# A state-space layer beside a Mish feed-forward: the third block's second product by seven quarter products over 16 of its 28 K tiles

## The chip, the core and the metric

The kernel runs on one core of a Trainium2 chip. The metric is the device time of one execution in microseconds (us), the median of several runs. Everything below is the work of five engines with one instruction queue each: PE (TensorE, matrix products, with PEld for its weight loads), DVE (VectorE), ACT (ScalarE), POOL (GpSimd, here mostly an issuer of DMAs) and SP (SyncE, an issuer of DMAs). The engines wait for one another through semaphores. PSUM, where PE accumulates, has eight banks of 128 x 512 float32.

## The reference, cut to what matters

```python
xn  = layernorm(x)                                  # x: 2048 x 1024, bf16
# S5: a diagonal complex recurrence over the 2048 rows
Bu  = xn @ B_bar.T;   h[t] = Lam_bar * h[t-1] + Bu[t]
y   = 2 * real(h @ C.T) + xn * Dskip
# feed-forward with Mish, F = 3584
hid = xn @ w1 + b1;   act = hid * tanh(softplus(hid))
out = x + y + act @ w2
```

`act @ w2` is called dense 2 here. Its K dimension is F = 3584, that is 28 K tiles of 128.

## The kernel before, in words

**Blocks.** The 2048 rows are worked in four blocks (`blk` 0 to 3) of 512 rows. Each block has three stages on PE: the products that make `hid` and the recurrence's input (L853, L929, L1001, L1361), dense 2 (L1415, in the last block L1472), and the projection of the recurrence's states by C (L1415 with `hT` as operand, L1438, L1446). All eight PSUM banks hold one block's output, 4 groups of 128 rows (`q`) by 2 halves of 512 columns (`h`): bank 2q + h. Dense 2 and the projection accumulate into the same banks, and DVE then adds the block's rows of x and puts the result into `xx` (L1545, L1541), which ACT sends out (L1531).

**Dense 2 in blocks 0 to 2.** For each K tile, eight matmuls of 128 x 128 by 128 x 512, one for each bank: 224 in a block. A ring of seven slots of 512 KB holds the right operands. SP loads it by a list (`items`): a slot gets the item seven places on as soon as PE (`item_done`) is through with it. A w2 item holds two K tiles, so it feeds 16 matmuls.

**Dense 2 in the last block.** There the product is done by seven quarter products (a Winograd form of Strassen's scheme) over K tile pairs: rows of the block are halved (th) and so are K (tile k and tile k + 14, "hi") and the columns. `KIND` = (1, 7, 2, 5, 6, 3, 4) is their order. Products 1, 2 and 4 take quarters of `act` as they are, products 5, 6, 7 and 3 take sums of quarters (S1, S2, S3, S4; `act_sums`, L1291, on DVE in float16). The right operands are quarters of w2 and sums of them (L1206, DVE); those are made once, group by group (`d2_load` L1173, `d2_row`/`d2_scale` L1186 on ACT, `d2_store` L1178 by POOL), where a group `g` is K tiles 2g, 2g + 1 and their partners, and go through DRAM (`w2d`). Seven groups make 28 K tiles. So that the float16 sums are in range, rows of w2 are scaled by powers of two (`row_sizes` L1222 and `row_powers` L1228 to L1232 find them), act by their inverses times a global power (`act_scale` L882; `row_bound`, `row_most`, `row_scales` find it through DRAM), and the states by the global power (L1389). ACT puts products 1, 7, 5 and 6 aside into `KS` (`keep`, L1483), and the end adds them back.

**What orders the work.** Every engine runs its queue in program order. For the first stages of blocks 1, 2 and 3 that order is written out by hand in the strings `WHOLE`, `STEPS` and `LAST`: two-letter steps, of which `p` to `z` are the products of w1 (`w_product`, `w_evacuate` with L1021 on ACT, L1024 and L1038 on DVE), `a` to `d` those of B, `r` the rotation of the states into the recurrence's frame (L891, L897, L899), `g` Mish (`mish`, L876), `k` one pending sum of w1 or w2 (L1151, L1206), `u` a first part of dense 2, `G` an `act_scale` of two tiles, `t` act sums, `m` and `h` load and scale w2 groups, `S` `row_scales`, `l` loads the next block's x. The recurrence (`recur`) then runs j = 0 to 7 on DVE: two scans (L1377), a rotation (L891) and two sums (L1384, L1386).

**The statistics of the next block's rows** (`next_stats`, `next_root`, `next_scale`) run on ACT during the recurrence, and SP transposes the result into `xnT` (`transpose_dma`).

## Time and profile before

| | |
|---|---|
| median of 3 runs | 591.79 us (591.69 to 592.7) |
| span of the profiled execution | 589.9 us (the page gives this span as its own time; the median lies 1.9 us above it) |
| PE busy | 586.5 us, 99% |
| DVE, ACT, POOL busy | 494.2, 384.6, 159.9 us |
| mean granted TensorE clock | 1.000 |
| block 2 on PE: first stage, dense 2, projection | 307.0 to 373.5, to 422.7, to 450.3 us |
| block 3 on PE: first stage, dense 2, projection | 450.3 to 516.7, to 559.9, to 587.7 us |

The times of the blocks are starts of the matmul groups in the trace, from the start of the span. A row of the timeline reads: start, length, engine, line, operation, out<-in, partitions x elements and type, count, and in brackets how long the engine was idle before it and who ended that.

### The profile page before, as it was taken

The numbers are of one execution on the slowest core, as the hardware profiler recorded it, in microseconds if no ns is written. First come the engines' busy times: TensorE is split into PE (matmuls) and PEld (weight loads), VectorE is DVE, ScalarE is ACT, GpSimd is POOL, SyncE is SP. The second block draws the span as 40 slices with busy tenths as digits, with TensorE's granted clock in tenths as the row PEclk, the third lists the DMA queues.
The fourth block names the chain that finished last, engine by engine and source line by source line (L and its number), as shares of the span: only waits on it lengthen the run. The fifth ranks groups of instructions, "written<-read, shape, count | busy, mean of one in ns | idle before, by whom it ended". The sixth has DMA issues, their size and how long they took to land.

```text
span 589.9 us, 9744 instructions
## 1 busy us (share of the span) xinstructions
PE 586.5 (99%) x3651; PEld 355.8 (60%) x3651; DVE 494.2 (84%) x730; ACT 384.6 (65%) x517; POOL 159.9 (27%) x225
## 2 busy tenths in 40 slices
PE   9999999999999999999999999999999999999998
PEld 8644444444447887444458888644446888844444
DVE  6999788999898778989737867998598669789996
ACT  4839994579577775992706477898342798892420
POOL 2899300213752213400302511144210123100000
PEclk9999999999999999999999999999999999999999
DMA  8999999997799688968869959999897966989832
GB/s 255 298 242 245 229 193 231 314 384 222 212 371 306 247 287 302 319 221 213 274 230 380 408 183 295 350 331 276 304 270 263 393 246 233 331 307 334 290 120 71
DMA packets 115993, 161.90 MB, mean 274 GB/s; under 512 B 56010, under 2 KB 67018, under 8 KB 115946
## 3 DMA queue, kind: packets, MB, share of 16 engines
q1 hardware_dynamic: 96768, 104.42, 59.3%
q0 software_dynamic: 14112, 46.28, 22.9%
q10 hardware_dynamic: 5066, 10.57, 5.0%
q8 instruction: 29, 0.48, 0.4%
q14 instruction: 18, 0.15, 0.1%
HBM read 115.09 MB, written 34.08 MB: 253 GB/s over the span
## 4 chain that ended last, share of the span: by engine, by line
PE 98%; DMA 1%; SPq 1%; DVE 0%; issue 0%
PE ps L1415 43%; PE ps L1001 19%; PE ps L929 12%; PE ps L853 10%; PE ps L1472 7%; PE ps L1361 5%; DMA ring<-in_B_w_dram 1%; PE ps L672 1%; PE ps L663 0%; PE ps L1438 0%; SPq L397 0%; PE ps L1446 0%; PE ps L505 0%; SPq L447 0%; SPq L401 0%; DVE xx L1572 0%
## 5 line engine op out<-in xcount | busy, mean ns | idle before, releaser
L1415 PE MATMUL ps<-ring,act 128*128 128x512 bf16 x672 | 145.9, 379 | 0.0
L1415 PEld LDWEIGHTS ps<-ring,act 128*128 128x128 bf16 x672 | 65.7, 98 | 78.4
L1021 ACT ACTIVATE snaps<-ps,par,cs 128x256 f32<-128x256 f32 x98 | 53.4, 562 | 54.4 <-PE ps L1001 29.3
L1415 PE MATMUL ps<-ring,hT 128*128 128x512 bf16 x370 | 80.3, 379 | 0.0
L1001 PE MATMUL ps<-TT,ring 128*128 128x256 f16 x576 | 71.2, 273 | 0.0
L891 DVE TENSOR_TENSOR mt<-hT,tab 128x2048 bf16<-128x2048 bf16 (+1 forms) x56 | 68.5, 1223 | 1.4
L1415 PEld LDWEIGHTS ps<-ring,hT 128*128 128x128 bf16 x370 | 36.2, 98 | 43.7
L1178 POOL DMA_DIRECT2D w2d<-hb x42 | 29.9, 714 | 117.2 <-DVE hb L1206 71.2
L1001 PEld LDWEIGHTS ps<-TT,ring 128*128 128x128 f16 (+1 forms) x576 | 56.2, 98 | 7.5 <-issue 0.2
L1038 DVE SCALAR_TENSOR_TENSOR act<-ps,cs,snaps 128x512 bf16<-128x512 f32 x54 | 40.1, 749 | 23.1 <-PE ps L1001 21.3
L1377 DVE TENSOR_TENSOR_SCAN hT<-cs,qi,hT 128x512 bf16<-128x512 f32 x48 | 58.9, 1269 | 0.0
L853 PE MATMUL ps<-xnT,ring 128*128 128x512 bf16 x264 | 57.3, 379 | 0.0
L1001 PE MATMUL ps<-xnT,ring 128*128 128x256 bf16 x432 | 54.5, 273 | 0.0
L1001 PEld LDWEIGHTS ps<-xnT,ring 128*128 128x128 bf16 (+1 forms) x432 | 42.3, 98 | 5.3
L853 PEld LDWEIGHTS ps<-xnT,ring 128*128 128x128 bf16 x264 | 25.8, 98 | 30.9
L876 ACT ACTIVATE act<-act 128x2048 bf16<-128x2048 bf16 (+3 forms) x12 | 32.8, 2756 | 6.9 <-DVE act L1024 6.8
L1130 POOL DMA_DIRECT2D wsd<-hb x35 | 18.9, 543 | 59.4 <-DVE hb L1151 35.1
L954 DVE TENSOR_TENSOR hT<-ps,snaps 128x512 f16<-128x512 f32 x36 | 23.9, 688 | 12.5 <-ACT snaps L946 10.2
L1136 ACT ACTIVATE hb<-hb,cs 128x2048 bf16<-128x2048 bf16 x10 | 19.4, 1993 | 19.9 <-DVE cs L1125 13.5
L861 ACT ACTIVATE act<-ps,par 128x512 bf16<-128x512 f32 (+1 forms) x40 | 23.9, 654 | 10.5 <-PE ps L853 10.5
L1361 PE MATMUL ps<-xnT,BT 128*128 128x512 bf16 x128 | 27.8, 379 | 0.0
L1415 PE MATMUL ps<-CT,hT 128*128 128x512 bf16 x128 | 27.8, 379 | 0.0
(223 smaller groups left out, 988.9 us busy)
## 6 DMA issues: line engine op xcount, KB each, us to landing
ring<-wsd SPq DMA_DIRECT2D x126, 256.0 KB, 5.3
ring<-in_B_w_dram SPq DMA_DIRECT2D x62, 512.0 KB, 5.6
ring<-ctd SPq DMA_DIRECT2D x24, 512.0 KB, 4.6
ring<-w2d SPq DMA_DIRECT2D x24, 512.0 KB, 4.7
w2d<-hb POOLq DMA_DIRECT2D x42, 256.0 KB, 5.2
wsd<-hb POOLq DMA_DIRECT2D x35, 256.0 KB, 5.1
hb<-in_B_w_dram POOLq DMA_DIRECT2D x20, 256.0 KB, 5.6
ctd<-CT ACTq DMA_DIRECT2D x8, 512.0 KB, 6.4
```

Of the source, the lines that this page charges most:

```text
L853: PE.mm(lambda e, k=k, w=w: e.matmul(ps[:, bank, :], lhsT=w, rhs=xnT[:, k, :], start=k == 0, stop=k == NK - 1), reads=[b_ring[s]] + b_xnT, ...
L876: aop(lambda e: e.activation(t, t, AF.Mish), reads=b, writes=b)
L891: vop(lambda e: e.tensor_tensor(mt[:], u.unsqueeze(1).to_broadcast([P, 2, 2, TB]), tab[:, :, j, :].unsqueeze(2).to_broadcast([P, 2, 2, TB] ...
L929: PE.mm(lambda e, w=w, x=x, o=o, begin=begin, end=end: e.matmul(ps[:, bank, o:o + TH], lhsT=w, rhs=x, start=opens and begin, stop=end, ski ...
L1001: PE.mm(lambda e, w=w, x=x, o=o, begin=begin, end=end: e.matmul(ps[:, bank, o:o + TH], lhsT=w, rhs=x, start=opens and begin, stop=end, ski ...
L1021: aop(lambda e, o=o, p=p, j=j: e.activation(o, p, AF.Identity, scale=ig, bias=b1(f0 + j)), reads=[b_ps[b], b_par, b_ig], writes=b_dst)
L1038: vop(lambda e: e.scalar_tensor_tensor(out=dst, in0=bank(b), scalar=ig, in1=src, op0=ALU.mult, op1=ALU.add), reads=[b_ps[b], b_snap[k], b_ ...
L1178: PO.dma(lambda e: e.dma_start(w2d[at // 4][:, at % 4 * TB:(at % 4 + 2) * TB].rearrange("p (j t) -> p j t", j=2), t[:, :, d, :]), sem, rea ...
L1361: PE.mm(lambda e, j=j, ci=ci, k=k, bank=bank: e.matmul(ps[:, bank + ci, :], lhsT=BT[:, ci, j, k, :], rhs=xnT[:, k, :], start=k == 0, stop= ...
L1377: vop(lambda e, ci=ci, init=init: e.tensor_tensor_scan(out=hT[:, ci, j, :], data0=cj("r", j).to_broadcast([P, TB]), data1=hT[:, ci, j, :], ...
L1415: PE.mm(lambda e: e.matmul(ps[:, u, :], lhsT=lhsT, rhs=rhs, start=st_, stop=last, skip_group_check=blk == NB - 1), reads=reads, writes=[b_ ...
L1472: PE.mm(lambda e: e.matmul(ps[:, bank, :], lhsT=lhsT, rhs=rhs, start=st_, stop=end, skip_group_check=True), reads=[b_t, b_ring[s]], writes ...
```

## The change

**Block 2's dense 2.** 16 of its 28 K tiles (groups 0 to 3: tiles 0 to 7 and 14 to 21) go through the seven quarter products, 8 tile pairs each, two matmuls for each pair. The other 12 tiles (`PLAIN`) are multiplied as before, eight matmuls for each tile, between products 6 and 3. The ring gets "tp" items for them, two DMAs of 256 KB from `w2d`, each item with four quarter tiles, which feed 8 matmuls.

**The w2 groups.** Four groups are now made before that: group 0 and 1 in block 1's recurrence (0 in the free parts of CT, 1 in `act`), group 3 in block 1's first stage, group 2 in block 2's first stage. Groups 4, 5 and 6 follow, for block 3 alone. All row sizes of w2 are taken in block 0 (14 items and not 10), and the sizes of w1's groups 0 and 1 ahead of the next block's square root; group 2's by ACT in block 0.

**The sums of act** for block 2 are written over quarters of `act` that are no longer needed (S1, S2, S4), S3 over CT.

**Block 2's end.** Its states are scaled like block 3's (`recur`), its products 1, 7, 5 and 6 are put aside by ACT and added back by DVE, and `uncarry` takes the scale from the state that block 3 starts with.

**The scans.** In all blocks the scans of later j stand between the rotation and the sums of j.

```diff
-    STEPS = ("p1 p5 p2 q1 q5 k0 k0 p6 q2 s1 k0 p7 s5 p3 k0 q6 s2 k0 p4 q7 k0 q3 k0 s6 q4 k0 m3 k0 g0 a2 a1 k0 s7 s3 k0 b2 b1 k0 s4 g1 m2 l0 a5 "
-            "b5 a6 b6 a3 b3 a7 b7 c2 d2 a4 b4 c5 c1 d5 d1 h12 r0 c6 c3 h13 d6 d3 h14 c7 h15 w1 d7 r1 w5 w2 c4 d4 w6 x1 x5 x2 k0 w7 k0 w3 r2 "
-            "x6 w4 y1 y5 y2 k0 x7 k0 x3 y6 A0 x4 z1 z5 g2 h8 h9 h10 M1 z2 y7 y3 z6 B0 h11 y4 z3 z7 u0 u2 r7 u1 z4 u7 r3 g3 r4 r6 r5")
+    NFG = {2: 4, 3: GF}
+    PLAIN = [(f, f + 1) for f in (*range(2 * NFG[2], NF // 2, 2), *range(NF // 2 + 2 * NFG[2], NF, 2))]
+    STEPS = ("p1 p5 p2 q1 q5 k0 k0 p6 q2 S0 s1 p7 s5 p3 m2 k0 q6 s2 k0 p4 q7 k0 q3 k0 s6 q4 k0 k0 g0 a2 a1 k0 s7 s3 k0 b2 b1 k0 s4 g1 a5 "
+            "b5 a6 b6 a3 h8 b3 a7 h9 b7 c2 d2 h10 a4 b4 h11 c5 c1 d5 d1 r0 c6 G0 c3 G1 d6 d3 c7 G2 w1 k0 d7 r1 w5 w2 G3 c4 d4 k0 w6 x1 x5 x2 k0 w7 k0 w3 r2 "
+            "x6 w4 y1 y5 y2 x7 x3 y6 x4 l0 z1 z5 g2 z2 y7 y3 z6 G7 y4 z3 z7 u0 t0 G8 u2 r3 z4 I2 G9 u1 g3 G10 t1 "
+            "r4 r5 t2 r6 r7")
...
+        elif blk in SPLIT:
+            units = [("tp", 7 * p + i) for p in range(7) for i in range(0, NFG[blk], 2)]
+            items += units[:5 * NFG[blk] // 2] + [("w2", (4 * REAL[f // 4] + f % 4) // 2) for f, _ in PLAIN] + units[5 * NFG[blk] // 2:]
...
+        def dense_part():
+            for n in KIND:
+                for k in range(2 * NFG[blk]):
+                    for i in range(2):
+                        if n != 1 and (n, i) != (7, 0):
+                            fast(n, i, k)
+                    if n != 1 and k % 4 == 3:
+                        item_done()
+                if n in (1, 7, 5, 6):
+                    keep({1: 2, 7: 0, 5: 1, 6: 3}[n], BANKS[n])
+                    for f in {1: (8, 10), 7: (12, 22), 6: (24, 26)}.get(n, ()):
+                        act_scale(blk, f // 2)
+                if n == 6:
+                    yield
+                    for fs in PLAIN:
+                        for us in ((4, 6, 1, 3, 5, 7), (0, 2)):
+                            for f in fs:
+                                dense(f, n_item[0] % NRING, us, fs == PLAIN[0] and f % 2 == 0)
+                        item_done()
...
+    def recur(blk, j):
+        if j == 0:
+            scan(blk, 0, 0)
+            scan(blk, 0, 1)
+            scan(blk, 1, 0)
         turn(hT[:, :, j, :], [b_hT[0][j], b_hT[1][j]], j)
+        if j + 1 < NJ:
+            scan(blk, j + 1, 1)
...
+        if j + 2 < NJ:
+            scan(blk, j + 2, 0)
-        if blk == NB - 1:
+        if blk in SPLIT:
             aop(lambda e: e.activation(hT[:, :, j, :], hT[:, :, j, :], AF.Copy, scale=wz[:, 2:3]),
...
+        if blk == FAST:
+            d2_load(0)
             for q in range(NQ):
                 next_stats(blk + 1, q)
+            for i in range(2):
+                w_abs(i)
...
+                if j == 3:
+                    w_scale(2)
+                if j == 5:
+                    w_exponent(1)
+                    w_scale(0)
+                    w_scale(1)
+                    row_bound()
+                if j == 6:
+                    some(4)
+                    d2_scale(1)
...
+        if blk == SPLIT[0]:
+            uncarry()
         if blk == FAST:
+            some(4)
             for i in (0, 1, 2):
                 w_sums(i, True)
+            some(2)
```

283 lines of the change are left out of this document (151 added, 132 removed), and 8 rows, old and new, of tables (LAST, WHOLE).

## The prediction

> **What bounds the kernel now.** I read the page first, then PE's waits, then the timelines of the stretches that the change touches.
>
> ```profile
> span 589.9 us, 9744 instructions
> PE 586.5 (99%) x3651; PEld 355.8 (60%) x3651; DVE 494.2 (84%) x730; ACT 384.6 (65%) x517; POOL 159.9 (27%) x225
> PEclk9999999999999999999999999999999999999999
> PE 98%; DMA 1%; SPq 1%; DVE 0%; issue 0%
> ```
> ```profile
> PE ps L625 <- DVE filler L457: 1.0, 1, 1.0
> PE ps L663 <- DMA ring<-in_B_w_dram: 0.2, 1, 0.2
> ```
>
> PE is busy for 99% of the span, the chain that ended last is PE for 98%, and the whole list of PE's waits is two lines, both from the start: 1.2 us. So a matmul less saves its full pace, if what PE then reaches earlier is ready; a wait put in front of PE costs itself. DVE at 84% and ACT at 65% matter only where they hand something to PE.
>
> **The change: PE.** Block 2's start, its dense 2, block 3's start, and the pattern that is taken over from block 3:
>
> ```profile
> 306.98 1.04 PE L1001 MATMUL ps<-xnT,ring 128*128 128x256 bf16 x8
> 373.46 4.05 PE L1415 MATMUL ps<-ring,act 128*128 128x512 bf16 x18
> 378.22 44.62 PE L1415 MATMUL ps<-ring,act 128*128 128x512 bf16 x206
> 422.69 27.79 PE L1415 MATMUL ps<-ring,hT 128*128 128x512 bf16 x128
> 450.31 1.04 PE L1001 MATMUL ps<-xnT,ring 128*128 128x256 bf16 x8
> 516.72 3.62 PE L1472 MATMUL ps<-ring,act 128*128 128x512 bf16 x16
> 520.17 1.04 PE L1001 MATMUL ps<-TT,ring 128*128 128x256 f16 x8
> 523.63 6.21 PE L1472 MATMUL ps<-ring,SA 128*128 128x512 f16 x28
> 529.68 6.21 PE L1472 MATMUL ps<-ring,act 128*128 128x512 bf16 x28
> ```
>
> Before: 18 + 206 = 224 matmuls. 206 of them take 422.69 - 378.22 = 44.47 us, 0.2159 each. After: 7 products x 8 pairs x 2 = 112, and 12 plain tiles x 8 = 96, so 208. The float16 products run at the same pace in block 3 (28 in 529.68 - 523.63 = 6.05 us, 0.2161 each), so the kind of operand changes nothing. No other matmul is added or removed; PE's instructions go from 3651 to 3635. **16 x 0.2159 = 3.45 us less.** All else is whether something makes PE wait.
>
> **The hand-over into block 2's dense 2** is tightest. The order on PE becomes: product 1's 16 matmuls from 373.46, the last w1 product (`z4`) from 373.46 + 3.45 = 376.91, then product 7 from 377.78 (`z4` takes 378.22 - 377.35 = 0.87, 377.35 being 373.46 + 18 x 0.2159), product 2 from 381.24. Product 2's last two pairs (383.83 and 384.26) read tiles 20 and 21, which ACT scales last, after Mish of the last four tiles, which waits for DVE's evacuation of `z4`. Block 3 has just this chain:
>
> ```profile
> 518.04 1.82 DVE L1291 TENSOR_TENSOR SA<-act 128x1536 f16<-128x1536 bf16 x2
> 521.25 1.12 DVE L1024 TENSOR_SCALAR act<-ps,cs,par 128x256 bf16<-128x256 f32 x2 [1.39 <-PE ps L1001]
> 525.48 1.22 DVE L891 TENSOR_TENSOR mt<-hT,tab 128x2048 bf16<-128x2048 f16 x1
> 527.52 1.22 DVE L891 TENSOR_TENSOR mt<-hT,tab 128x2048 bf16<-128x2048 f16 x1
> ```
> ```profile
> 522.41 3.62 ACT L876 ACTIVATE act<-act 128x4096 bf16<-128x4096 bf16 x1 [1.39 <-DVE act L1024]
> 526.05 5.01 ACT L882 ACTIVATE act<-act,cs 128x512 bf16<-128x512 bf16 x8
> 530.97 2.39 ACT L1483 ACTIVATE KS<-ps,wz 128x512 f32<-128x512 f32 x4
> ```
>
> There the scaling starts 526.05 - 520.17 = 5.88 us after the product, and each tile takes (530.97 - 526.05)/8 = 0.615. Here it starts at 376.91 + 5.88 = 382.79; tile 20 is ready at about 383.50 and tile 21 at 384.1, 0.33 and 0.15 us before PE. DVE has more ahead of that evacuation than block 3: S1 (1.82 by the row, started like there 518.04 - 516.72 = 1.32 after the first product, at 374.78; 0.91 + 0.34 for the shares due here) and one rotation (527.52 - 525.48 = 2.04), so it is free at 378.07, where the evacuation could start at 376.91 + 521.25 - 520.17 = 377.99: 0.08 late. The margin left is under 0.1 to 0.25 us, so I put **0.1 us** on this term; its bounds are 0 and, if DVE or ACT come 2 us later (one rotation), about 2. Behind it ACT puts the products aside at 2.39/4 = 0.60 a bank, with the scaling of four more tiles (2.46) after product 1 and after product 7: 384.1 + 2 x (1.2 + 2.46) = 391.4, and product 5 is aside 1.2 later, at about 392.5. The plain part starts on other banks at 381.24 + 3 x 3.45 = 391.60 and needs product 5's at its sixth matmul, 392.68; product 6's banks are aside near 393.2 and 393.7 and needed at the thirteenth, 394.19. These 0.2 to 0.5 us are thin too.
>
> **The ring.** SP's list gets 14 "tp" items of two DMAs in place of 8 items of one, and the item that was 16 matmuls (3.45 us) is now 8 (1.73). That is block 3's pace from block 3's tensor. Landings of the ring's loads there (510 to 545), and of w2 itself around 364 to 374:
>
> ```profile
> DMA to landing us min/median/max: 4.3/4.8/6.4
> DMA to landing us min/median/max: 4.4/6.1/9.9
> ```
>
> The shortest lead that I find in block 2 is that of the seventh "tp" item: its slot comes free at about 377.9 (just behind `z4`) and it is used by the fourth product, at 381.24 + 3.45 = 384.69, 6.8 us. 6.4 fits, so I take 0; at 9.9 PE would wait 3.1.
>
> **Blocks 0 and 1.** The work for the new groups is off PE; what it could delay is a block's end.
>
> ```profile
> 106.53 1.15 ACT L814 ACTIVATE ct<-CT,cs 128x1024 f32<-128x1024 bf16 x1 [1.73 <-DVE CT L816]
> 113.35 1.15 ACT L814 ACTIVATE ct<-CT,cs 128x1024 f32<-128x1024 bf16 x1 [2.13 <-DVE CT L816]
> 120.17 1.15 ACT L814 ACTIVATE ct<-CT,cs 128x1024 f32<-128x1024 bf16 x1 [4.35 <-DVE CT L816]
> 126.99 1.15 ACT L814 ACTIVATE ct<-CT,cs 128x1024 f32<-128x1024 bf16 x1 [1.23 <-DVE CT L816]
> ```
> ```profile
> L1222 ACT ACTIVATE hsink<-ring 128x1024 bf16<-128x1024 bf16 x20 | 21.1, 1054 | 1.0
> L1377 DVE TENSOR_TENSOR_SCAN hT<-cs,qi,hT 128x512 bf16<-128x512 f32 x48 | 58.9, 1269 | 0.0
> ```
> ```profile
> 158.99 4.62 DVE L1545 TENSOR_TENSOR xx<-ps,xx 128x1024 bf16<-128x1024 f32 x4 [1.62 <-PE ps L1415]
> 419.92 2.94 DVE L1206 TENSOR_TENSOR act<-act 128x1024 f16<-128x1024 bf16 x4 [9.48 <-DMA w2d<-act]
> 437.93 0.42 DVE L1386 TENSOR_TENSOR hT<-mt 128x512 bf16<-128x512 bf16 x1
> 574.37 4.62 DVE L1552 TENSOR_TENSOR KS<-KS,xx 128x1024 f32<-128x1024 f32 x4
> 292.43 0.17 DVE L1402 TENSOR_TENSOR qi<-qi,qt 128x8 f32<-128x8 f32 x1
> 302.00 1.23 DVE L1545 TENSOR_TENSOR xx<-ps,xx 128x1024 bf16<-128x1024 f32 x1 [9.40 <-PE ps L1415]
> ```
>
> Block 0: eight more row sizes on ACT, 8 x 1.05 = 8.4 us, in a stretch where it idles 1.73 + 2.13 + 4.35 + 1.23 = 9.4 for DVE. What spills over reaches DVE's end by about 1 us, and there DVE waited 1.62 for PE: 0. Without that cover it would cost that 1 us.
>
> Block 1: group 3's four sums, 2.94 us by the row of such sums at 419.92, and about 1.3 of small work put DVE's recurrence later by some 4 us: before it was done with the block at 292.6 and then idled 9.40 for PE, now at about 296.7. There stand, ahead of the evictions, group 1's four sums and two of w1. The sums are written over their sources, so they wait for the landing of the raw stores. ACT's last scaling of the stretch and POOL's last issue stood at 294.5 before, and the page lists such stores with 5 us to landing:
>
> ```profile
> 294.48 0.54 POOL L1130 DMA_DIRECT2D wsd<-act x1 [0.81 <-ACT act L1136]
> ```
> ```profile
> wsd<-act POOLq DMA_DIRECT2D x3, 256.0 KB, 5.0
> ```
>
> So the last raw store lands at about 299.6; two of the four sums are left then, 1.4 us, and the two of w1, 1.4: evictions from 302.4 instead of 302.00. They need to start by 306.98 - 1.23 = 305.75 (the first bank's next use, where block 2 begins). 3.3 us of margin: 0.
>
> **Block 2's recurrence and end.** DVE loses 12 w2 sums (three times 2.94) and the 9.48 us wait that stood ahead of the last four, and gains its act sums and KS sums: the last `hT` comes near 429.5 rather than 438.35, and ACT scales it by 433.7; PE needs it at about 440 (the projection starts at 422.69 - 3.45 = 419.24, and I take its last quarter, 32 of the 128 matmuls, as what reads it). Then on DVE the next block's x and TT (as before, 8 us), the small state work, four KS sums (4.62 by 574.37): evictions from about 443.2. They must start by 450.31 - 3.45 - 1.28 = 445.6: 2.4 us of margin, 0. The scans' new order can save DVE at most 0.06 us a j (1269 ns in the group against about 1.23 a scan), and DVE waits for PE at each block's end: 0. Block 3 keeps its order.
>
> **The sum**: 589.9 - 3.45 + 0.1 = 586.55 of span; the median lies 1.9 above the span, so 591.79 - 3.35 = **588.4 us**.
>
> **The rivals.**
> A. *ACT's and DVE's hand-over becomes PE's bound* at 383 to 394. For it: margins of 0.1 to 0.5 us in four places in a row. Against: block 3 runs the same chain, and PE there never waits. One rotation late is 2.04 us, so 588.5 + 0.5 to 2 = 589 to 590.5.
>
> B. *Slower: the w2 sums ahead of block 1's evictions wait for their raw stores.* For it: the same four sums stood 9.48 us idle for the same stores in block 2 (row at 419.92). If group 1's wait as long from 296.7, they start at 306.2, end at 309.1, the two of w1 at 310.5, the first eviction at 311.7: PE, which wants the bank at 306.98, waits 4.75 us, and 588.4 + 4.75 = 593.1. It decides from the end of the sums: past 309.2 the gain is gone, past 310.4 the kernel is slower. Against: such stores land after 5.0 us here, and ACT is done with its scaling near 294; whether block 2's were issued late or landed late, these rows don't say.
>
> A PE that idles this long may also come back slowly. The trace's only case is the start:
>
> ```profile
> 2.94 1.22 PE L503 MATMUL ps<-ident,xx 128*128 128x128 bf16 x8
> 12.62 0.61 PE L505 MATMUL ps<-ident,xn 128*128 128x128 bf16 x8
> ```
>
> The same eight matmuls take 1.22 us at 2.94 and 0.61 at 12.62: half pace, then full. [...]
>
> C. *The gain is given back to a late ring load*: a "tp" item that lands after 9.9 us, as the slowest w2 load near there did, makes PE wait 3.1: 591.4, no change.
>
> **How the numbers follow.** About 0.2% (1.2 us) is what a measurement of this kernel can tell from no change. Forecast (588.0 to 588.8): 0.65. A: 0.14, C: 0.09, B: 0.12. A is faster still (up to 590.5 < 590.6), so faster 0.79, same 0.09, slower 0.12. The range leaves out B and the upper end of C: from 587.9 (no hand-over loss, and a run at the low end of those shown, 0.1 less and rounding) to 591.2.
>
> **What would show it.** In the changed profile: dense 2 of block 2 takes 208 matmuls and the projection starts near 419.3; block 2's first product at 306.98 as before; PE's waits still two lines. Wrong by A: waits of PE in 383 to 394 put down to ACT's scaling or its putting aside. Wrong by B: PE's first products of block 2 waiting for DVE's evictions, and DVE for `w2d<-act`. Wrong by C: PE waiting for the ring from `w2d`. Wrong altogether: a pace of the new matmuls over 0.216.

## The result and the profile after

The changed kernel takes **610.71 us** (median of 4 runs, 608.35 to 613.48) against 592.10 us for the kernel before, measured beside it (4 runs, 591.69 to 592.7): a ratio of 1.0319 (95% interval 1.0283 to 1.0354). The forecast was 588.4 us, faster; the kernel is 3.2% slower. Some executions lie over 1.5% above the fastest of their version: the ratios of the experiments below leave these out (that of e4 does not), and the profiled executions of e1 and e3 are such ones, read for places and not for sizes.

The page of the changed kernel, the lines that answer to those of before:

```profile
span 607.9 us, 9804 instructions
PE 588.6 (97%) x3635; PEld 354.5 (58%) x3635; DVE 499.3 (82%) x739; ACT 416.2 (68%) x565; POOL 160.6 (26%) x229
PEclk9999999999999999999869999999999999999999
PE 79%; DMA 10%; DVE 4%; ACT 3%; POOL 2%; issue 1%; SPq 1%; ACTq 0%
```

PE has its 3635 instructions, 16 fewer, as forecast. But the chain that ended last is now PE for 79% and DMA for 10% (before 98% and 1%), and the clock's row shows one dip, 8 and 6 tenths in slices 20 and 21 of 40, that is from 289 us on. PE's timeline around it (start, length, work, and in brackets the idle time before it):

```profile
161.70 20.88 PE L866 MATMUL ps<-xnT,ring 128*128 128x512 bf16 x96
...
293.16 3.61 PE L1460 MATMUL ps<-ring,hT 128*128 128x512 bf16 x16 [2.42 <-DVE CT L1232]
300.23 6.45 PE L1460 MATMUL ps<-ring,hT 128*128 128x512 bf16 x16 [3.46 <-DVE xx L611]
315.65 12.48 PE L1460 MATMUL ps<-ring,hT 128*128 128x512 bf16 x48 [8.97 <-DMA ring<-ctd]
327.98 1.04 PE L1015 MATMUL ps<-xnT,ring 128*128 128x256 bf16 x8
...
468.06 1.03 PE L1015 MATMUL ps<-xnT,ring 128*128 128x256 bf16 x8
```

The row of before for the first product of block 1:

```profile
161.38 20.88 PE L853 MATMUL ps<-xnT,ring 128*128 128x512 bf16 x96
```

The three rows that begin a block give the balance. **Block 2** lasts 468.06 - 327.98 = 140.08 us against 143.33 before: 3.25 us less, where 3.35 was forecast. **Block 1** lasts 327.98 - 161.70 = 166.28 us against 145.60: 20.68 us more, where 0 was forecast. Block 0 is 0.32 us longer in this execution. So the loss stands in block 1, and nearly all of it in its projection, which takes 20.1 us longer (from 280.22 to 327.98, before from 279.35 to 306.98).

Of the 20.7 us, 2.42 + 3.46 + 8.97 = 14.9 us are the waits in brackets. Another 5.0 us are pace: 16 matmuls take 6.45 us instead of 3.45, and the 48 from 315.65 to 327.98 take 12.33 us instead of 10.36. The last 0.8 us are small pieces. The stretches of that time (length, PE, PEld, DVE, ACT, POOL, granted clock, DMA share, GB/s):

```profile
300.00:310.00 10.00, 6.45 (x16) 2.21 (x16) 2.70 (x5) 0.00 (x0) 1.29 (x2) 0.67 1.07 146
310.00:316.00 6.00, 0.34 (x1) 0.14 (x2) 1.91 (x4) 0.00 (x0) 0.58 (x1) 0.50 1.03 363
316.00:323.00 7.00, 7.00 (x25) 2.79 (x24) 3.84 (x12) 0.00 (x0) 1.37 (x2) 0.74 0.99 373
```

The granted clock is 0.67, 0.50 and 0.74 there. In shorter stretches it is 0.50 behind the wait of 3.46 us (300.2 to 303.5) and behind that of 8.97 (315.6 to 318), and 1.00 again from 321 to 324; behind the wait of 2.42 us it is 1.00 (293.1 to 296.8), and the 16 matmuls take 3.61 us, so nearly full pace. The prediction's trace had a slow stretch of PE only at the start of the program, where the granted clock reads 1.00 (2.9 to 4.2 us). The DMA share in the three rows above is full (0.99 to 1.07; the measure can exceed 1), although from 300 to 310 us only 146 GB/s move, against 363 and 373 behind it. What held the packets back there, no run shows.

What PE waited for begins much earlier. From the chain of waits of the changed kernel between 244 and 316 us, its three DMA pieces:

```profile
244.54 10.51 DMA w2d<-hb
257.57 6.51 DMA hb<-in_B_w_dram
294.88 20.63 DMA ring<-ctd
```

POOL's queue holds the last store of w2 group 3 (`w2d<-hb`), and the load of a w1 group goes to the same place in `hb`, so it waits for that store to land. ACT takes that group's sizes (L1113) ahead of the root of the next block's statistics. The root is late, the four transposes of the next block's rows are late, and they then stand among the stores of the new groups. SP's issue of the transposes and of the loads of `ctd` (C, PE's operand in the projection) between them, before and after (start, length):

```profile
262.78 1.24 SPq L603 DMA_TRANSPOSE xnT<-xn  x1
...
273.11 2.80 SPq L603 DMA_TRANSPOSE xnT<-xn  x1
```
```profile
274.94 1.24 SPq L615 DMA_TRANSPOSE xnT<-xn  x1
...
278.50 1.80 SPq L459 DMA_DIRECT2D ring<-ctd  x1
280.39 7.14 SPq L615 DMA_TRANSPOSE xnT<-xn  x1
287.63 1.23 SPq L459 DMA_DIRECT2D ring<-ctd  x1
288.95 5.80 SPq L615 DMA_TRANSPOSE xnT<-xn  x1
294.88 2.77 SPq L459 DMA_DIRECT2D ring<-ctd  x3
```

The transposes start 12 us later, and two of them hold SP's queue for 7.14 and 5.80 us with `ctd` loads behind them. The time to landing of the first two of these loads (min, median, max of a stretch with that one load each):

```profile
DMA to landing us min/median/max: 14.5/14.5/14.5
```
```profile
DMA to landing us min/median/max: 12.5/12.5/12.5
```

278.50 + 14.5 = 293.0 and 287.63 + 12.5 = 300.1: PE goes on at 293.16 and 300.23. So the two waits that the profile puts down to DVE are the ring's as well, like the third (294.88 + 20.63 = 315.51, and PE at 315.65); DVE's last `hT` was done by 297.2, and PE needed it later. The queues' traffic from 245 to 325 us (packets, MB, share of 16 engines; q1 is SP's, q0 POOL's), before and after, with the median time to landing of all eight `ctd` loads:

```profile
q1 hardware_dynamic: 10967, 15.60, 62.4%
q0 software_dynamic: 1505, 4.84, 16.4%
...
ring<-ctd SPq DMA_DIRECT2D x8, 512.0 KB, 4.3
```
```profile
q0 software_dynamic: 3588, 11.58, 51.8%
q1 hardware_dynamic: 8325, 10.80, 44.0%
...
ring<-ctd SPq DMA_DIRECT2D x8, 512.0 KB, 13.5
...
w2d<-CT POOLq DMA_DIRECT2D x7, 256.0 KB, 13.1
```

The stores that the prediction priced, group 1's raw ones, are the three that POOL issues from 299.17 to 300.6 us (with their median time to landing):

```profile
w2d<-act POOLq DMA_DIRECT2D x3, 256.0 KB, 15.3
```

POOL moves 11.58 MB in place of 4.84, the two queues fill 95.8% of the engines' time and not 78.8%, and the same loads take 13.5 us to land and not 4.3. Group 0's stores take 13.1 us and group 1's raw ones 15.3, where the prediction took 5.0. DVE's waits in the changed kernel:

```profile
273.26 0.18 DVE L597 RECIPROCAL ln<-ln 128x4 f32<-128x4 f32 x1 [10.42 <-ACT ln L595]
...
314.05 0.69 DVE L1745 TENSOR_TENSOR TT<-xnT 128x1024 f16<-128x1024 bf16 x1 [11.14 <-DMA xnT<-xn]
320.40 2.94 DVE L1232 TENSOR_TENSOR act<-act 128x1024 f16<-128x1024 bf16 x4 [2.88 <-DMA w2d<-act]
```

It stands 10.42 us for the root and 11.14 us for the transposes. For the raw stores that rival B named it stands only 2.88 us, because it comes to them so late: the last lands at 320.4 us.

### The profile page after: what moved, and what is told of

Read it like the earlier page. It is cut to its first block, busy times and chain, and to the rows that moved or that the text cites. A ratio compares the mean times of both kernels' runs of the same rounds, so it can differ in the third digit from the quotient of the medians.

```text
span 607.9 us, 9804 instructions
## 1 busy us (share of the span) xinstructions
PE 588.6 (97%) x3635; PEld 354.5 (58%) x3635; DVE 499.3 (82%) x739; ACT 416.2 (68%) x565; POOL 160.6 (26%) x229
## 4 chain that ended last, share of the span: by engine, by line
PE 79%; DMA 10%; DVE 4%; ACT 3%; POOL 2%; issue 1%; SPq 1%; ACTq 0%
PE ps L1460 26%; PE ps L1015 17%; PE ps L943 12%; PE ps L1519 11%; PE ps L866 6%; PE ps L1396 5%; DMA ring<-ctd 3%; DMA w2d<-hb 3%; DMA act<-in_B_w_dram 1%; DMA ring<-in_B_w_dram 1%; ACT xn L1113 1%; DVE hT L1411 1%; DMA hb<-in_B_w_dram 1%; PE ps L684 1%; ACT hb L1154 1%
## 5 line engine op out<-in xcount | busy, mean ns | idle before, releaser
L1460 PE MATMUL ps<-ring,act 128*128 128x512 bf16 x544 | 118.1, 379 | 0.0
L1460 PE MATMUL ps<-ring,hT 128*128 128x512 bf16 x362 | 83.9, 395 | 14.8 <-DMA ring<-ctd 9.0
L1460 PEld LDWEIGHTS ps<-ring,act 128*128 128x128 bf16 x544 | 53.2, 98 | 63.7 <-ACT KS L1534 0.2
L1411 DVE TENSOR_TENSOR_SCAN hT<-cs,qi,hT 128x512 bf16<-128x512 f32 x48 | 60.8, 1276 | 0.0
L1204 POOL DMA_DIRECT2D w2d<-hb x28 | 20.0, 716 | 81.9 <-DVE hb L1232 45.0
L1519 PE MATMUL ps<-ring,act 128*128 128x512 bf16 (+1 forms) x180 | 40.0, 379 | 0.0
L1431 ACT ACTIVATE hT<-hT,wz 128x1024 bf16<-128x1024 bf16 x16 | 18.1, 1144 | 20.6 <-DVE hT L1426 20.6
L1247 ACT ACTIVATE hsink<-ring 128x1024 bf16<-128x1024 bf16 x28 | 29.5, 1054 | 1.4
L1519 PEld LDWEIGHTS ps<-ring,act 128*128 128x128 bf16 (+1 forms) x180 | 17.6, 98 | 20.6 <-ACT act L896 0.3
```

What stands on the lines that cost most here:

```text
L1247: aop(lambda e, src=src, r=r: e.activation(hsink[:], src, AF.Abs, accum_out=wp[:, r:r + 1]), reads=[b_ring[s]], writes=b_hbf[2 * GF:] + [b ...
L1411: vop(lambda e: e.tensor_tensor_scan(out=hT[:, ci, j, :], data0=cj("r", j).to_broadcast([P, TB]), data1=hT[:, ci, j, :], initial=init, op0 ...
L1460: PE.mm(lambda e: e.matmul(ps[:, u, :], lhsT=lhsT, rhs=rhs, start=st_, stop=last, skip_group_check=blk in SPLIT), reads=reads, writes=[b_p ...
L1519: PE.mm(lambda e: e.matmul(ps[:, bank, :], lhsT=lhsT, rhs=rhs, start=st_, stop=end, skip_group_check=True), reads=b_t + [b_ring[s]], write ...
```

## The experiments

Three theories run through the expectations. One is that the late root by itself makes the loss. The second is that the work does: DVE's and ACT's instructions for the new groups are too much for block 1, in whatever order. The third, Theory 3 in the expectations from e5 on, is that transfers do: SP's transposes and ring loads stand beside POOL's new loads and stores, all become slow, and what waits for their landing waits. Times are medians with the lowest and highest run; "before" is the median of the kernel before, measured beside each; "block 1, 2, 3" are the starts of those blocks on PE in the profiled execution.

| run | us | before | ratio (95%) | block 1 | block 2 | block 3 |
|---|---|---|---|---|---|---|
| before | 592.10 (591.69-592.7) | | | 161.38 | 306.98 | 450.31 |
| changed kernel | 610.71 (608.35-613.48) | 592.10 | 1.0319 (1.0283-1.0354) | 161.70 | 327.98 | 468.06 |
| e1 | 609.18 (607.34-619.21) | 591.15 | 1.0279 (1.0238-1.0321) | 171.07 | 335.67 | 478.15 |
| e2 | 591.11 (590.72-594.2) | 591.15 | 0.9996 (0.9976-1.0016) | 161.31 | 306.91 | 450.25 |
| e3 | 620.87 (607.33-627.64) | 591.15 | 1.0268 (1.0218-1.0318) | 179.93 | 340.00 | 482.09 |
| e4 | 613.03 (607.27-618.26) | 591.15 | 1.0355 (1.0279-1.0431) | 164.35 | 324.47 | 466.45 |
| e5 | 600.16 (596.58-605.0) | 591.04 | 1.0151 (1.0107-1.0194) | 166.63 | 317.14 | 458.76 |
| e6 | 592.60 (590.8-598.39) | 591.04 | 1.0036 (1.0008-1.0065) | 161.29 | 306.89 | 450.23 |
| e7 | 594.96 (591.34-604.97) | 591.46 | 1.0033 (0.9990-1.0076) | 161.26 | 309.60 | 452.95 |
| e8 | 591.33 (590.67-601.63) | 591.46 | 0.9994 (0.9960-1.0029) | 161.30 | 307.01 | 450.35 |
| e9 | 593.45 (590.9-599.5) | 591.46 | 1.0044 (1.0011-1.0077) | 161.38 | 308.45 | 452.62 |
| e10 | 601.18 (599.42-605.57) | 591.93 | 1.0168 (1.0125-1.0210) | 161.06 | 306.98 | 459.17 |
| e11 | 598.37 (594.74-602.18) | 591.58 | 1.0112 (1.0071-1.0154) | 161.09 | 307.05 | 453.94 |
| e12 | 598.41 (593.34-601.1) | 591.58 | 1.0092 (1.0059-1.0125) | 161.19 | 315.03 | 456.98 |
| e13 | 595.05 (592.54-606.16) | 591.39 | 1.0052 (1.0020-1.0083) | 161.01 | 310.29 | 452.63 |
| e14 | 593.33 (591.69-596.53) | 591.39 | 1.0026 (1.0004-1.0047) | 161.16 | 310.52 | 452.37 |
| e15 | 608.10 (605.01-612.33) | 591.39 | 1.0268 (1.0216-1.0320) | 161.03 | 326.33 | 469.29 |
| e16 | 589.65 (587.98-596.86) | 591.39 | 0.9967 (0.9941-0.9994) | 160.93 | 307.05 | 447.57 |

### Is it the late root? e1 to e4

e1, the changed kernel with the sizes of w1's groups behind the root and the scaling, so that the root no longer waits for a load (all edits from here on are cut to what matters):

```diff
@@ block 1, ahead of the recurrence
-            for i in range(2):
-                w_abs(i)
@@ behind next_root() and next_scale()
+                    for i in range(2):
+                        w_abs(i)
```

> The changed kernel with one move undone: ACT takes the sizes of w1's groups 0 and 1 behind the next block's square root and its scaling of xn, as the kernel before does, and not ahead of them (their scratch output goes to tiles 8 to 15 of act). Theory 1 (the square root waits for ACT's sums of w1, those for a load that waits for group 3's stores; the late root puts the transposes into the stretch in which w2 is stored, and the load of C's rows stands behind them): ACT does the root near 253, DVE does not idle 10.4 us at the reciprocal, the transposes are issued near 263 to 275 as before, and PE's 9.0 us wait for ring<-ctd is gone. But the sizes are then ready later still, near 284, and DVE waits for them ahead of j = 6, so some of PE's other two waits (2.4 and 3.5) may stay: 589 to 594 us. Theory 2 (the added stores and loads of w2 alone overfill the DMA queues at 280 to 315, whatever the root does): the wait for ring<-ctd stays, 600 us or more.

The time hardly moves: 609.18 us. The waits at `ctd` went, and others came. DVE and PE of e1:

```profile
330.11 2.94 DVE L1232 TENSOR_TENSOR act<-act 128x1024 f16<-128x1024 bf16 x4 [10.13 <-DMA w2d<-act]
```
```profile
335.67 1.86 PE L1015 MATMUL ps<-xnT,ring 128*128 128x256 bf16 x8 [17.69 <-DVE xx L1619]
```

Group 1's sums stand 10.13 us for their raw stores ahead of the evictions, and PE waits behind them: the mechanism of rival B, but here only, where the sizes, and with them the scalings and stores, come later.

e2, the kernel before with the sizes of w1's groups moved ahead of the root, as the change has them:

```diff
+            for i in range(3):
+                w_abs(i)
...
-                    w_abs(0)
-                    w_abs(1)
-                    w_abs(2)
```

> The kernel before with this one move made: ACT takes the three sums of w1 ahead of the next block's square root. No work of the new groups is there, and the loads of w1 are issued by 246. By theory 1 the sums find their data landed, so the root is late only by the sums' own 3 x 3.8 = 11.4 us less what DVE does meanwhile; DVE has 9.4 us to spare at the end of the block and the transposes move to 272 to 285, ahead of most stores: 592 to 595 us. If a root 10 us late is in itself worth what the changed kernel lost (about 20 us), 605 us or more: then no group 3 is needed for it.

0.9996: this later root costs nothing without the change's traffic on POOL's queue (11.58 MB from 245 to 325 us in the changed kernel, 4.84 in the kernel before). But it is not as late as the changed kernel's: the first transpose starts at 267.05 us here, 4.3 us later than before and not 12. What the full lateness is worth, e14 below settles.

e3, the changed kernel with w2 group 3 made earlier in block 1's first stage, so that its stores are out of the way (in `WHOLE`, steps h13, h14, h15 and the k0 behind them moved forward):

```diff
-              "... h12 p7 ... s1 s5 h13 c4 ... w6 h14 s3 w3 s7 h15 w7 r2 u4 s4 w4 r3 k0 u5 l0 k0 u6 u7 g4 r4 k0 g5 ..."
+              "... h12 h13 p7 ... h14 h15 s1 s5 c4 ... w6 s3 w3 s7 w7 r2 k0 k0 u4 s4 w4 k0 k0 r3 u5 l0 u6 u7 g4 r4 g5 ..."
```

> The changed kernel with group 3 of w2 scaled and summed earlier in block 1's first stage: ACT's four scalings two by two at about 206 and 217 instead of 205, 221 and 228, DVE's four sums ahead of the third rotation instead of between the last ones, so that POOL issues the last store near 233 and not 244.5. ACT's sums of w1 stay ahead of the root. Theory 1: the load of w1's group 0 is issued near 242 and not 255, ACT finds it landed, the root comes near 262, DVE hardly waits, and PE waits nowhere in block 1: 588 to 590 us, the forecast of the blind prediction. Theory 2 (sums ahead of the root are bad by themselves, or the added traffic is): still over 595.

The root comes earlier (DVE's wait falls from 10.42 to 4.05 us), and the time does not fall: two of the six runs take 607.33 and 608.44 us (the ratio goes by these), four take 618.86 to 627.64. The profiled one of these four began block 1 only at 179.93 us, after waits of PE for the ring in block 0, which pointed to a second place.

e4, e3 with the scans in the order of before:

```diff
-        if j == 0:
-            scan(blk, 0, 0)
-            scan(blk, 0, 1)
-            scan(blk, 1, 0)
+        scan(blk, j, 0)
+        scan(blk, j, 1)
```

> The previous kernel (group 3 earlier) with the two scans of each j back ahead of its rotation, as in the kernel before. Prediction's term: the order of the scans is worth at most 0.06 us a j on DVE, and DVE is off the path: within 0.5 us of the previous run. Rival: the spread of the scans is what keeps DVE in time, then PE waits in block 1 or 2 and it is 1 us or more slower.

The four runs fall into the same two groups: 607.27 and 608.66 us, 617.40 and 618.26. The lower two agree with e3's lower two within 0.3 us, so the scans' order is worth nothing that these few runs show. (The table's 1.0355 is only reached with the longer two.)

### Is it the collision of transfers? e5 and e6

e5, the changed kernel with POOL quiet while SP transposes: group 3 as in e3, w1 group 1's load earlier, group 1's w2 load and all scalings and their stores behind those of w1's groups 0 and 1, group 1's sums behind the evictions:

```diff
-                    d2_load(1)
-                    d2_scale(0)
-                if j == 3:
-                    w_scale(2)
-                if j == 5:
+                if j == 4:
                     w_exponent(1)
                     w_scale(0)
+                    d2_load(1)
                     w_scale(1)
                     row_bound()
-                if j == 6:
-                    some(4)
+                    d2_scale(0)
+                    w_scale(2)
                     d2_scale(1)
```

> The changed kernel with POOL's queue emptied where the transposes of block 1 run: group 3 scaled and summed earlier, as in the run that did that alone; w1's group 1 loaded ahead of its stores; the load of w2's group 1 and the scalings, and so the stores, of w2's groups 0 and 1 and of w1's group 2 put behind those of w1's groups 0 and 1 (from about 274 on); group 1's four sums moved behind the block's evictions. The work is the same. Theory 3: the transposes run at 265 to 277 with little beside them, no wait of PE for ring<-ctd is left, and the 16 matmuls come through: 588 to 590 us. If the root's lateness or the amount of traffic is what costs, it stays over 596.

600.16 us: half of the loss is back (9.1 us over before, where the changed kernel was 18.6 over). Block 1's projection runs unbroken and block 2 follows it at once (the trace lacks three of its 128 matmul records):

```profile
289.52 27.79 PE L1460 MATMUL ps<-ring,hT 128*128 128x512 bf16 x125
317.14 1.04 PE L1015 MATMUL ps<-xnT,ring 128*128 128x256 bf16 x8
```

Block 1 lasts 150.51 us and not 166.28. But it starts at 166.63: five microseconds are lost in block 0.

The stretch from 245 to 325 us of this trace, where block 1 is 5 us later, shows that it is not the amount of traffic:

```profile
q0 software_dynamic: 3632, 11.74, 47.0%
ring<-ctd SPq DMA_DIRECT2D x8, 512.0 KB, 5.8
```

POOL moves as much as in the changed kernel (11.74 and 11.58 MB), and yet the `ctd` loads land after 5.8 us and not 13.5, and SP issues the four transposes in 1.24 to 3.14 us each, where two took 7.14 and 5.80 in the changed kernel. So it is what stands beside the transposes that differs, not the sum over the stretch.

e6, the other way round: the kernel before, with 12 stores of 256 KB to a scratch tensor on POOL's queue behind the first two sizes of w1, while SP transposes:

```diff
+                        for n in range(6):
+                            PO.dma(lambda e, i=i, n=n, t=t: e.dma_start(
+                                dum[6 * i + n], hb[:, t:t + 2, :].rearrange("p f t -> p (f t)")),
+                                sem, reads=b_hbf[t:t + 2] + [b_wsm[0][i]])
```

> The kernel before, and twelve stores of 256 KB by POOL that nothing needs (of w1's rows in hb, to a scratch tensor in DRAM): six behind ACT's first sum of w1 in block 1 and six behind its second, so that they run at 262 to 275 us, beside the four transposes of the next block's rows and the loads of C's rows. [...] Theory 2b (POOL's stores are harmless to SP's queue; the changed kernel is late by its chain of waits on DVE and ACT): within 1 us of the kernel before, since DVE has 9.4 us to spare at the end of block 1.

The transposes become slow, up to 7.30 us each (1.24 to 2.80 before), so the collision is real. But the kernel before has room for most of it: 1.0036, and its profiled execution had no wait of PE behind its first 12 us. (That execution took 591.09 us; four of the ten took 594.64 to 598.39, and no trace shows why.) Neither forecast held, 596 us or more by Theory 3 and within 1 us of before by its rival. 3.1 MB of stores alone don't make the loss; in the changed kernel they come on top of loads, sums that wait for them, and a recurrence that is already late.

### Block 0: e7 to e9

Two things of the change stand in block 0: eight more row sizes on ACT, and a broadcast of w1's row maxima that has five columns and not four (320 KB against 256 KB), which POOL sends while SP transposes C. In e5 one of those transposes takes 7.28 us (issued alone, such ones take 1.31):

```profile
68.92 7.28 SPq L841 DMA_TRANSPOSE CT<-in_A_C_im_dram  x1
```

ACT's first scaling of C starts at 100.79 us there, and at 96.10 before.

e7, e5 without the sizes of items 10 to 13 (a constant stands in their place):

```diff
-                for g in ((7,), (8,), (9, 10), (11, 12, 13))[j]:
+                for g in ((7,), (8,), (9,), ())[j]:
```

> The kernel is the quiet-transposes kernel (600.16 us) without the row sizes of items 10 to 13 in block 0: eight ACTIVATEs of 1.05 us with their reads of 0.19 us, 9.9 us of ACT. Left out of the computation: the sizes of rows of w2 of those four items, which are set to a constant. Theory S (block 0's remaining loss is the eight sizes: ACT has no slack left between C's scalings, holds ring slots, and every lateness reaches the evictions): block 1's first product comes at 161.3 to 162 us instead of 166.6, PE has no wait at DVE's evictions of block 0, and the time falls by 6 to 9 us, to 591 to 594 us. Theory W (the loss is made earlier, by the 320 KB broadcast of w1's row maxima, 64 KB larger than before, that runs beside the transposes of C): the first C scaling stays at 99 to 101 us rather than 96, and block 1 starts 3 to 5 us late with or without the eight sizes; the time falls by 0 to 3 us only. Both may hold together: C late, but the freed slack of ACT absorbs it; then as by S.

e8, the kernel before with all 14 items sized in block 0:

```diff
-            if j < 3:
-                row_sizes(0, j + 7)
+            if j < 4:
+                for g in ((7,), (8,), (9, 10), (11, 12, 13))[j]:
+                    row_sizes(0, g)
```

> The kernel before with the eight more row sizes of block 0, placed as the change places them, and nothing else of the change (their results are overwritten later). Theory S alone: ACT's slack of 9.4 us in that stretch is used up, block 1's first product comes 1 to 5 us after 161.38 us and the time rises by 1 to 6 us. Theory W, or S and W only together: without the larger broadcast C's scalings start at 96 us, ACT just manages, block 1 starts within 0.7 us of before, and the time is 591.5 to 593 us.

e9, e5 with the broadcast behind the transposes:

```diff
-            if f == 26:
-                w_row(0)
...
-                w_exponent(0)
+            if j == 6:
+                w_exponent(0)
...
                 for i in range(NHS):
                     rows_load(i)
+                w_row(0)
```

> The quiet-transposes kernel with the store and the broadcast of w1's row maxima behind the loads of B's rows in block 0 (from j = 3 on, to another place in act) and the exponents at j = 6; all sizes as the change has them. Theory W: no transpose of C is issued beside the broadcast, the second one takes 1.3 to 3 us and not 7.28, the first C scaling starts at 95 to 97.5 us and not 100.8, block 1's first product at 161.5 to 163 us, and the time falls by 4 to 8 us, to 592 to 596 us. Theory S: C's scalings start earlier, but ACT still has 9.9 us more to do between them and the ring waits for it; block 1 starts at 164 us or later, and the time falls by 0 to 3 us. If slow transposes of B at 45 us (4 to 10 us each in the kernels so far) are the larger part, the runs scatter as before by several us.

In e7 C is still late (first scaling at 100.42 us), yet block 1 starts at 161.26; in e9 C is in time (95.47 us) and block 1 starts at 161.38 with all sizes in place; in e8 the sizes alone cost nothing (0.9994). So in e5 it takes both: beside the broadcast C comes some 4 us late, and the sizes have used up the slack of ACT that would have absorbed it. Taking away either one brings 5 to 7 us (600.16 to 594.96 and 593.45, measured at different times). "Both together", which e7's expectation allowed for, is what holds. Two things stay open. That the 64 KB more are what makes C late isn't shown: e9 moves the whole broadcast, and in e8 one transpose beside the smaller one takes 4.55 us. And the loss is on the brink: the changed kernel's own profile has C at 99.74 us, all sizes in place, and block 1 still begins at 161.70.

### Does an order remove the rest? e10 to e12

e9 loses another 2.0 us against before instead of gaining 3.4: two ring waits in block 1's first stage, and PE waiting 2.16 us at block 2's start for group 0's sums, which lie where the evacuations write.

e10, e9 with group 0 scaled and stored first, and w1 group 1 loaded later (`d2_raw` issues the raw stores and queues the sums, which the end of `d2_scale` did for group 0 until here):

```diff
+                if blk == FAST:
+                    d2_scale(0)
@@ behind w_exponent(1)
+                    d2_raw(0)
                     w_scale(0)
@@ in WHOLE
-              r2 n1 k0 k0 u4 s4 w4 k0 k0 r3 u5 l0 u6 u7 n0
+              r2 k0 k0 u4 s4 w4 k0 k0 r3 u5 l0 u6 u7 n1 n0
```

> The kernel with the row maxima behind the transposes (593.45 us, block 1 from 161.38, block 2 from 308.45, block 3 from 452.62 us), with two steps moved: ACT scales w2 group 0 (4.25 us) right behind the scaling of the next block's rows, where it was idle for 6.22 us, and POOL sends its quarters ahead of those of w1; and w1 group 1 is loaded behind the last sums of group 3. Nothing is left out. Theory 3 (all that the change loses are collisions and waits at transfers; its saving on PE in block 2 is real): DVE's wait of 8.66 us for group 0's raw stores goes, the stores of its sums land before block 2's first evictions, so ACT's and DVE's waits at the snaps (19.67 and 2.67 us) no longer hold PE (2.16 us), the two ring waits at 230 us (1.1 us) go; block 2 starts at 307 to 307.5 us, block 3 140 to 141 us later, and the time is 588 to 590 us, under before by 1.5 to 3.5 us. Rival (the seven quarter products' extra work on DVE, ACT and POOL is too much for block 1 wherever it stands): another wait of 2 us or more takes their place, and the time stays at 592 us or above.

This expectation failed by 12 us. Block 2 starts at 306.98, as before, and then PE waits 9.96 us: POOL's queue held group 0's finished sums behind the fetch of the global maximum.

```profile
307.61 0.58 POOL L1278 DMA_DIRECT2D qmx<-qmd  x1 [6.20 <-DMA qmd<-wz]
308.19 2.84 POOL L1204 DMA_DIRECT2D w2d<-CT  x4
```

e11, e10 with those sums and their stores at j = 6, and w1 group 1 sized before group 0; e12, e11 with w1 group 1's load where e9 had it:

```diff
                     row_bound()
+                if j == 6:
+                    some(4)
                     w_scale(2)
```

> The kernel before this one (group 0 first, 601.18 us) with the four sums of w2 group 0 and their stores emitted at j = 6, so that POOL has them ahead of group 1's stores and of the fetch of the global maximum, and with w1 group 1's sizes taken ahead of group 0's (its load lands first). Theory 3 (a queue's order decides, not the amount of work): POOL sends the four sums at 290 to 294 us rather than from 308.19 us (where they stood behind the fetch that waited 6.20 us), ACT and DVE no longer wait for them at the snaps beyond block 2's start (20.74 and 11.88 us now), PE's wait of 9.96 us goes; the time is 588.5 to 592 us. Rival (the extra stores are too many for block 1 wherever they stand): PE waits 3 us or more in block 1 or at block 2's start, and the time stays above 593 us.

> As the kernel with group 0's sums at j = 6, but with the load of w1 group 1 ahead of the last sums of group 3 again, where it cost two ring waits of 0.38 and 0.75 us in block 1's first stage. Theory 3: those two waits come back, the root comes 2 to 4 us earlier than with the late load, and the two kernels are within 2 us; this one is 589 to 593 us. Rival as above.

In e11 block 2 again starts in time (307.05), and PE then waits 4.9 us in three pieces for `wsd`, its next operand; the first:

```profile
312.75 3.58 PE L1015 MATMUL ps<-TT,ring 128*128 128x256 f16 x16 [2.05 <-DMA ring<-wsd]
```

In e12 the wait of 4.5 us at `ctd` is back. The rivals' side of these three expectations held: each order removed its wait and found the next. But e9 to e12 all keep the stores, and none loses as the changed kernel does. That left work against transfers open.

### Work or transfers? e13 to e16

e13, the changed kernel without the 14 stores of w2 groups 0 and 1 (3.7 MB); every load, scaling and sum stays, and the products read group 3's quarters in their place:

```diff
     def d2_store(g, n, h, d, sem):
+        if g < 2:
+            b_w2d[(KIND.index(n) * NF // 2 + 2 * g) // 2].writer = b_w2d[(KIND.index(n) * NF // 2 + 6) // 2].writer
+            return
...
+                v = v - v % 7 + 3 if v % 7 < 2 else v
```

> The changed kernel without the 14 stores of 256 KB of w2 groups 0 and 1; all their loads, scalings and sums stay, in the change's order. Left out of the computation: the quarters of these two groups, in whose place products read those of group 3 (in block 3 two loads of 256 KB stand for one of 512 KB). Traffic theory (what block 1 loses is transfers: 3.7 MB more of stores on POOL's queue beside the transposes and the ring, and waits for their landing): the wait of 3.46 us behind DVE and most of that of 8.97 us at the last ctd item go, block 2 starts 10 to 20 us earlier than the changed kernel's 327.98, and the time is 591 to 600 us against 610.71. Work theory (DVE's and ACT's work for the groups is too much for block 1): DVE's and ACT's instructions are all there, so block 2 still starts after 320 us and the time is 603 us or more.

e14 is e13 with e9's edit in block 0, and e15 is the changed kernel with that edit alone:

> The same without the 14 stores, and with the row maxima's broadcast behind the transposes of block 0, as in the kernel that had block 1 from 161.38 us. Left out: as there. Both losses taken away at once. Traffic theory: block 1 starts at 161 to 162 us, and the time is that without the stores less what block 0 costs there (0 to 4 us): 588 to 597 us, and in a run without any wait 588.4. Work theory: 602 us or more.

> The changed kernel with the row maxima's broadcast behind the transposes of block 0 and nothing else. If block 0 (the broadcast beside C's transposes, with no slack left on ACT) is a separate loss that only sometimes comes through in the changed kernel (its profiled run began block 1 at 161.70 us, its times spread over 608.35 to 613.48): block 1 begins at 161 to 162 us, the time is 606 to 610 us, and the block 1 loss of some 20 us stays in full. If the broadcast were the cause of block 1's loss too: under 600 us.

e16 is e11 with e13's edit:

> The kernel with group 0's sums at j = 6 and quiet transposes (598.37 us), without the 14 stores of groups 0 and 1. Left out: as in the changed kernel without them. Traffic theory: nothing of the four waits at ring loads of wsd (4.9 us in all) is left, since those loads stood beside the stores; block 2 starts at 307 us, lasts 140.1 us, and the time is 587.5 to 589.5 us: the saving of 3.4 us on PE shows. If some other transfer or the work itself stands behind those waits: over 592 us.

e13 gives back most of the loss, 595.05 us, with all of DVE's and ACT's work in place. The work theory asked for 603 us or more and falls. e15, e14, e9 and e16 share the edit in block 0, so block 1's length in their profiles separates its loss (145.60 us before):

| block 1, us | the change's order | a quieter order |
|---|---|---|
| with the 14 stores | 165.30 (e15) | 147.07 (e9) |
| without them | 149.36 (e14) | 146.12 (e16) |

**So neither is the cause alone: it takes the 14 stores in the change's order.** Leaving out the stores gives back 15.9 us, the quieter order with all stores 18.2, and both together 19.2. (e16's order is e11's, a few steps further than e9's.) Some of it comes back in block 2. Over blocks 1 and 2 the four take 308.26 (e15), 291.24 (e9), 291.21 (e14) and 286.64 us (e16), and the kernel before 288.93: either remedy alone gives back 17.0 us and ends above the kernel before, and only both end below it.

e14 also settles the late root. Its first transpose starts at 274.51 us, as late as in the changed kernel, and block 1 is 3.8 us longer than before, not 19.7. The runs don't separate the stores' traffic from the waits of DVE's sums for their landing. But what PE waited for in the changed kernel were `ctd` loads, and these land after 7.8 us in e14 and 5.7 in e9, not 13.5.

What e13 and e14 keep is DVE: its sums no longer wait for stores, but the late root has put its recurrence, and with it the evictions, later (they start at 308.93 in e13), and PE waits 3.4 and 3.6 us for them. In e16 the list of PE's waits is short again, and the saving shows:

```profile
PE ps L639 <- DVE filler L471: 1.0, 1, 1.0
PE ps L677 <- DMA ring<-in_B_w_dram: 1.0, 1, 1.0
PE ps L945 <- ACT act L876: 0.4, 1, 0.4
PE ps L1017 <- ACT snaps L1037: 0.3, 1, 0.3
```
```profile
307.05 1.04 PE L1017 MATMUL ps<-xnT,ring 128*128 128x256 bf16 x8
...
447.57 1.03 PE L1017 MATMUL ps<-xnT,ring 128*128 128x256 bf16 x8
```

Block 2 lasts 140.52 us against 143.33, and the kernel is 0.3% faster than before: 589.65 against 591.39 us, 0.9967 (0.9941 to 0.9994). It leaves the stores out, so it is no version to use; no complete version here beat the kernel before. Whether the 3.7 MB could go outside block 1 was not tried.

e15 at 608.10 us says what block 0 costs the changed kernel itself: 2.6 us by the medians (610.71 was measured at another time, and the two ratios' intervals overlap, so the size isn't settled), and next to none of block 1's loss.

## Why the prediction was wrong, point by point

**PE's term, right.** 3.45 us were forecast; block 2 is 3.25 us shorter in the changed kernel, and 2.81 us with 0.3 us of waits in e16.

**The hand-over, the ring and block 2's end (0.1, 0 and 0), right.** PE has no wait inside block 2 or at block 3's start in the changed kernel. Rivals A and C didn't come. The margin at block 2's end isn't sure, though: in e15's profile PE waits there 1.15 us for ACT's scaling of `hT` and 1.27 us for an eviction.

**The scans (0), not told apart** from nothing by e4.

**Block 0 (0), wrong by a few microseconds.** The step said that eight sizes of 1.05 us fit into 9.4 us of ACT's idle time. That alone held (e8). What it left out is the broadcast of w1's row maxima beside C's transposes, which the change makes one column wider: C comes some 4 us later, and the slack was spent twice. The loss scatters, by the author's estimate with how broadcast and transposes meet: block 1 began at 161.70 us in the changed kernel's profile and at 166.63 in e5's.

**Block 1 (0), wrong by 20.7 us, and this is the step that failed.** It read: "the page lists such stores with 5 us to landing", and ended at "3.3 us of margin: 0". It looked for the danger at the evictions alone, and put nothing on what the new groups' stores do to the transposes and to the ring's loads for the projection ahead of them. There PE lost its time: the `ctd` loads landed after 13.5 us and not 4.3, which cost 14.9 us of waiting and 5.0 of pace. The 5 us to landing were not a property of a store either: group 1's raw stores, issued 5 us later than forecast, took 15.3. The step also said "DVE's recurrence later by some 4 us", and didn't follow the step that moved: w1's sizes went ahead of the root, and their load stands on POOL's queue behind group 3's last store, so the root came 12 us later and the transposes fell among the stores. Stores and order make the loss together: without the 14 stores block 1 is 15.9 us shorter (e15 to e14), and with them in a quieter order 18.2 us (e15 to e9).

**Rival B, right in its sign and its block, not in its mechanism.** It had PE wait for evictions behind group 1's sums. In the changed kernel these waited 2.88 us, after PE had long lost its time to the ring. B itself is e1's row of 10.13 us. The lower clock (0.50 granted at first) took 3.0 us behind the wait of 3.46 and 2.0 behind that of 8.97.

## What to carry to other kernels

A transfer's time to landing held here only for the traffic in which it was measured: the `ctd` loads took 4.3 us in the kernel before. The bytes of a whole stretch didn't tell what it would be: with as many on POOL's queue the `ctd` loads landed after 13.5 us in the changed kernel and 5.8 in e5. So before adding stores, list which loads and transposes will be in flight beside them, and price each of those and each wait behind it anew. Slack is spent once: two edits that each fit into an engine's idle time can fail together (the sizes fit alone in e8, and fail in e5, where C comes late). To tell work from transfers, leave the transfers out and keep the work, and then test the order with the transfers in: only the table of both showed that the loss needs the two together.

## What the runs showed of the hardware

**Transposes beside stores.** SP's four transposes of the next block's rows land after 5.3 us (median) in the kernel before, 10.9 in e6, where only twelve stores are added, and 14.8 in the changed kernel. SP issues the first in 1.24 us before; it was held up to 7.30 us by one in e6 and 7.14 in the changed kernel. The traffic of the kernel before while transposes of C run alone, and of the changed kernel while that transpose of 7.14 us is issued:

```profile
DMA packets 1492, 0.37 MB, mean 288 GB/s; under 512 B 1492, under 2 KB 1492, under 8 KB 1492
```
```profile
DMA packets 1498, 2.20 MB, mean 305 GB/s; under 512 B 1018, under 2 KB 1018, under 8 KB 1498
q0 software_dynamic: 414, 1.44, 59.8%
```

Alone, SP's queue moves 1492 small packets in 1.3 us (0.37 MB, 250 bytes each). Beside POOL's 414 packets of 1.44 MB / 414 = 3.5 KB, 1018 small ones pass in 7.2 us: 7.1 ns each instead of 0.87. That is a rough size only, since the two windows are not alike: the first holds transposes out of DRAM back to back, the second those of `xn`, with 66 larger packets of SP's own loads among them. How the two queues share the engines, no run here shows.

**PE's clock** fell to 0.50 behind waits of 3.46 and 8.97 us within the changed kernel, as shown above, and not behind one of 2.42: 14.9 us of waiting cost 19.8.
